# First loads on ScalarE's queue, and K's transposes moved on VectorE: two attention blocks on one core

## The chip, the cores and the metric

The kernel runs on one core of a Trainium2 chip. The metric is the device time of one execution in microseconds. A core has TensorE (matrix products), VectorE, ScalarE, GpSimd, SyncE and 16 DMA engines. In the profile they are PE (with PEld, its weight loads), DVE, ACT, POOL and SP. A suffix q (SPq, ACTq) means the engine's instruction queue, mostly while it issues a DMA. The engines run on their own and wait for each other by semaphores. Each executes its own instructions strictly in order.

## What is computed

Two independent attention blocks, A and B, and their outputs side by side. For each block, with B = 16 batches, 64 queries, D = 640, H = 32 heads of 128, and 512 cached keys, all in bfloat16:

```python
q = (x @ wq).reshape(B, Sq, H, Dh).transpose(0, 2, 1, 3)
scores = einsum("bhqd,bhkd->bhqk", q, k_cache) * (Dh ** -0.5)
p = softmax(scores, axis=-1)
o = einsum("bhqk,bhkd->bhqd", p, v_cache)
out = o.transpose(0, 2, 1, 3).reshape(B, Sq, H * Dh) @ wo
```

K and V are read once: 268 MB of the 295 MB that the profile counts.

## The kernel before

**Packs.** The unit of work is a pack: four heads of two batches, so 128 rows (two times 64 queries) by four heads. Four packs (j = 0 to 3) share one pair of batches and its x. Eight pairs make a phase of 32 packs, for 16 heads. A block has two phases, the kernel four, so there are 128 packs, n = 0 to 127. Each phase has its own wq and wo columns for 16 heads. The sum over the two phases of a block is held in acc.

**Steps of a pack.** The names are those of the plan and of the functions em_... that write the instructions:

- LDK (four loads of 256 KB, rows of 8 KB), LDV (two loads of 512 KB, rows of 4 KB, or of 2 KB in every fourth pack): K and V into rings of 6 and 4 packs.
- LDX (160 KB, rows of 1,280 bytes): x of a pair. LDWQ: wq. In phase 0 it is cut by pack, four loads of 640 KB with rows of 1 KB; later phases have five loads of 512 KB with rows of 4 KB. LDWO: wo, 640 KB in rows of 1,280 bytes.
- XT, XE, XC: transpose x on TensorE, bring it out on ScalarE, copy it on GpSimd (L582, L588, L592). WP: GpSimd reorders wq of a pack, two copies (L575).
- QP, QE: the query product (TensorE, L603) and its way out (ScalarE, L609).
- KT: VectorE transposes K, in two halves (L617). S: scores (TensorE, L627).
- EX: exp of one head with its row sum (ScalarE, L646). RC: reciprocals, RC0 for heads 0 to 2 and RC1 for head 3 (VectorE, L659). NM: p times the reciprocal into pn_sb, four times (GpSimd, L675; for the last pack VectorE).
- TR: transpose pn_sb (TensorE, L686). TE: two copies of it to SBUF (VectorE, L696). PV: product with V (TensorE, L710). OE, ZO: its way out and a clearing of PSUM (ScalarE, L718, L722). OP: product with wo (TensorE, L730). OS: every fourth pack, add into acc or out_sb (VectorE, L740, L743). ST: store (ScalarE's queue, L749).

**What sets the order.** build_plan gives each step a planned time: the pack's number plus an offset from the table AT, in units of one pack. Each engine's program is its steps sorted by that time. Dependencies are also found in that order: a read depends on the last write planned ahead of it. SP is the exception: it only issues loads, sorted by the key that stands in `loads`. So an offset in AT is no delay. It says only what stands ahead of what. In TensorE's order, one pack is S(n), TR(n-1), OP(n-2), for some XT, QP(n+1), PV(n-1). TensorE runs this as a loop of 32 turns of four packs, whose program is written once.

**The first microseconds.** Packs -2 and -1 are dummies that run TR, PV and OP on cleared tiles. SP issues x0, wq0, K0, wq1, K1, wq2, K2, wq3, x1, V0, wo0, K3, V1, wo1, K4, V2, wo2, K5, V3, wo3, K6, x2, V4 and so on. V4 goes into the buffer that V0 had, so SP waits there until PV(0) is through; V5 waits for PV(1). Everything behind a waiting load on SP waits too. Between V4 and V5 stand two loads of the next wq (phase 1) and K7. GpSimd's order is WP(0), XC(0), WP(1), the clearing of pn_sb (L666) that TR(-1) needs, WP(2), NM of pack 0, WP(3), NM of pack 1.

**VectorE's order in one pack** is, by AT: RC0(n), sometimes OS, RC1(n), the two KT of pack n+2, the two TE of pack n, then RC0(n+1).

Of the kernel before, what the change touches and what calls it, by code (L numbers as in the profile page):

```python
# [20 lines left out]
class Cfg:  # L21
# [9 lines left out]
    BASE = 32  # L31
    KLEAD = 2.5
    WIDE = (0, 1, 2)
    AT = dict(XT=-2.485, XE=-2.28, XC=-0.9, QP=-0.45, QE=-0.24, KT=(-1.24, -1.0), S=0,
              EX=(0.21, 0.32, 0.43, 0.54), RC=(0.53, 0.75), NM=(0.56, 0.69, 0.82, 0.95), NMZ=(0.54, 0.55, 0.56, 0.76), TR=1.2,
              TE=(1.26, 1.39), PV=1.75, OE=(2.0, 2.06), ZO=2.11, OP=2.31, OS=2.545, LDWO=2.6, ST=3.374, WP0=-1.75, WP1=-1.6)


class Op:
# [19 lines left out]
def build_plan(dims, cfg, general):  # L59
# [6 lines left out]
    N = NPH * PH  # L66
    AT = cfg.AT
    ops = []
    loads = []
    at = {}  # L70

    def add(eng, kind, idx, ts, reads=(), writes=()):
        op = Op(eng, kind, idx, ts, reads, writes)
        ops.append(op)
        at[(kind, idx)] = op
        return op

    def add_output(n):
        g, j = n // NJ, n % NJ
        final = n >= 0 and dims["FINAL"](g // NBP)  # L80
        for b in range(2):
            tv = n + AT["PV"]
            op = add("sp", "LDV", (n, b), tv - 0.3, [], [("v" if n >= 0 else "absent", n % cfg.NV, b)])
            loads.append((n - cfg.NV + AT["PV"] + 0.2 if n >= 0 else -99.0, 3, op))
        if n > -2:
            add("pe", "TR", n, n + AT["TR"], [("pn", i) for i in range(4)] + [("ident",)], [("B", 4), ("B", 5)])
        for b in range(2):
            add("dve", "TE", (n, b), n + AT["TE"][b], [], [("B", 4 + b), ("pT", b)])
        add("pe", "PV", n, n + AT["PV"], [("pT", 0), ("pT", 1), ("v", n % cfg.NV, 0), ("v", n % cfg.NV, 1)],
            [("B", 4), ("B", 5), ("B67",)])  # L90
# [13 lines left out]
    for g in range(N // NJ + 1):  # L104
        n0 = g * NJ
        txt = n0 + AT["XT"]
        add("pe", "XT", g, txt, [("xn", g % cfg.NXN), ("ident",)], [("SB", 0)])
        if g == N // NJ:
            break
        if dims["FIRST"](g // NBP):  # L110
            add("act", "XE", g, n0 + AT["XE"], [], [("SB", 0), ("xs", g % NBP)])
            op = add("sp", "LDX", g, txt - 0.5, [], [("xn", g % cfg.NXN)])
            loads.append((txt - 3.7 if g else -7.0, 0, op))
        add("pool", "XC", g, n0 + AT["XC"], [("xs", g % NBP)], [("xT", g % cfg.NX)])
    for ph in range(NPH):
        twp = [ph * PH + j + (AT["WP1"] if ph else AT["WP0"]) for j in range(NJ)]
        for kt in range(dims["KT"] if ph else 0):
            ready = twp[-1] - PH + 0.5 if ph > 1 else NJ - 1 + AT["WP0"] + 0.5
            op = add("sp", "LDWQ", (ph, kt), twp[0] - 0.5, [], [("ws", kt, j) for j in range(NJ)])
            loads.append((ready + 0.5 + 0.5 * kt if ph == 1 else ready + 2.0 + 0.14 * PH * kt, 1, op))  # L120
        for j in range(NJ):
            w = ph * NJ + j
            n0 = ph * PH + j
            add("pool", "WP", w, twp[j], [("ws", kt, j) for kt in range(dims["KT"])], [("wqp", j)])
            if not ph:
                op = add("sp", "LDWQ", (0, j), twp[j] - 0.5, [], [("ws", kt, j) for kt in range(dims["KT"])])
                loads.append((0.9 * j - 5.2, 1, op))
            if ph:
                add("act", "LDWO", w, n0 - NJ + AT["LDWO"], [], [("wo", j)])
            else:  # L130
                loads.append((n0 - 1.9, 4, add("sp", "LDWO", w, n0 + AT["OP"] - 0.8 * NJ, [], [("wo", j)])))
# [6 lines left out]
    for n in range(-2, N):  # L138
# [3 lines left out]
        g, j = n // NJ, n % NJ  # L142
        add("pe", "QP", n, n + AT["QP"], [("xT", g % cfg.NX), ("wqp", j)], [("SB", 1)])
        add("act", "QE", n, n + AT["QE"], [], [("SB", 1), ("qs", n % cfg.NQ)])
        for i in range(4):
            op = add("sp", "LDK", (n, i), n + AT["KT"][0] - 0.9, [], [("kn", n % cfg.NK)])
# [6 lines left out]
        for i in range(4):  # L153
            h = 4 * n + i
            te = n + AT["EX"][i]
            if general:
                add("dve", "MX", h, te - 0.002, [], [("SB", i), ("negmax", h % 4)])
            add("act", "EX", h, te, [("negmax", h % 4)] if general else [],
                [("SB", i), ("p", h % cfg.NP), ("rs", h)])
# [4 lines left out]
    if not general:  # L164
        add("dve", "FL1", 0, N - 1 + AT["TE"][1] + 0.002, [("rs", h) for h in range(4 * N)], [("good",)])
        add("pe", "FLM", 0, N - 1 + AT["OP"] + 0.002, [("good",)], [("SB", 0)])
# [38 lines left out]
    for op in ops:  # L205
# [3 lines left out]
        if op.kind == "XT" and op.idx > 0:  # L209
            at[("EX", 4 * (NJ * op.idx - NJ + 1))].deps += [d for d in op.deps if d.kind == "LDX"]  # L210
            op.deps = [d for d in op.deps if d.kind != "LDX"]
        if op.kind == "QP" and op.idx > 0:
            at[("EX", 4 * op.idx - 4)].deps += [d for d in op.deps if d.kind == "WP"]
            op.deps = [d for d in op.deps if d.kind != "WP"]

    own = {"XC", "QE", "KT", "NM", "TE", "OE", "ZO", "OS", "LDV"}

    def for_pe(d):
        if d.kind == "EX":
            return d.idx % 4 < 2  # L220
        if d.kind == "OE":
            return d.idx[1] == 0
        if d.kind == "NM":
            return d.idx % 4 == 3 and d.eng == "pool"
        if d.kind == "OS" and d.idx == N // NJ - 1:
            return False
        return d.kind in own

    def stand_in(d, op):
        if op.eng == "pe":  # L230
# [4 lines left out]
            if d.kind == "OE":  # L235
                return at[("OE", (d.idx[0], 0))]
            if d.kind in ("EX", "MX") and not for_pe(d):
                if op.kind == "S":
# [11 lines left out]
        if d.kind == "OS":  # L250
            return at[("PV", d.idx * NJ + NJ)]
        if d.kind == "TE":
            return at[("PV", d.idx[0])]
# [9 lines left out]
    counts = dict(base)  # L263

    def sem_key(op):
        if op.kind == "LDV":
            return ("d_v", op.writes[0][1])
        if op.kind in LOADS:
            return ("d_" + op.kind[2:].lower(),) + op.writes[0][1:]
        if op.kind == "ST":  # L270
            return ("d_out",)
        return ("q_" + op.eng,) if for_pe(op) else ("s_" + op.kind.lower() + "_" + op.eng,)

    for eng in ENGINES:
        for op in progs[eng]:
            op.sem = sem_key(op)
            counts[op.sem] = op.count = counts.get(op.sem, 0) + 1
# [151 lines left out]
def mha_kernel(nc, blocks, out, cfg=None):  # L429
# [17 lines left out]
    for general in (False, True):  # L447
        dims = dict(NPH=NPH, NBP=NBP, NJ=NJ, KT=KT, FIRST=lambda ph: ph % NSUB == 0,
                    FINAL=lambda ph: ph % NSUB == NSUB - 1)
        plans.append(build_plan(dims, cfg, general))  # L450
# [457 lines left out]
```

## Time and profile before

| | |
|---|---|
| Median of 6 runs | 749.7 us (749.08 to 752.27) |
| The profiled execution | 749.43 us, its span 747.7 us |
| TensorE busy, granted clock | 678.3 us (91%), 0.99 |
| VectorE, ScalarE, GpSimd busy | 526.0, 519.0, 404.0 us |
| Moved by DMA | 295.15 MB, mean 395 GB/s over the span |
| GpSimd's NM waiting for RC | 315.2 us in 121 waits |
| VectorE's KT waiting for K | 78.2 us (B) and 37.9 us (A) |
| SP waiting for PV ahead of a V load | 36.1 us and 18.4 us |
| The chain that ended last | PE 40%, SPq 29%, DMA 12% |

How to read it: the span runs from the first to the last instruction. A timeline line has the start, the time that the group took, the engine with the line of the code, the operation, its output and inputs, the number of instructions, and in brackets the idle time ahead of it with what ended it. "issue" there means that the profile shows nothing that was waited for. In the table by windows the last two columns are the share of time that the DMA engines were busy (it can pass 1.00) and the rate.

### The profile page before, as it was taken

The page shows a single profiled execution, that of the slowest core. Times are in us where ns is not written, and L with a number is a line of the kernel's source. Part 1 is how long each engine was busy: PE and PEld are TensorE (multiplying, and loading weights), DVE is VectorE, ACT ScalarE, POOL GpSimd, SP SyncE. Part 2 cuts the span into 40 slices and gives each one's busy share as a digit, 9 for nine tenths or more (in the row PEclk, how much of TensorE's full clock was granted, in tenths as well). Part 3 has the DMA queues.
Part 4 walks back from the last instruction along what each step waited for, and adds up shares of the span by engine and source line. Part 5 has one row for each costly group of instructions (what it writes and reads, how often), then busy time and mean ns, then how long its engine had stood idle before and what let it go on. Part 6 is the DMA issues. An engine that isn't in the chain of part 4 may idle for free.

```text
span 747.7 us, 57618 instructions
## 1 busy us (share of the span) xinstructions
PE 678.3 (91%) x26518; PEld 530.7 (71%) x26518; DVE 526.0 (70%) x818; ACT 519.0 (69%) x1559; POOL 404.0 (54%) x580
## 2 busy tenths in 40 slices
PE   4579999999998999989988999999898899999994
PEld 3457777777776777777766777777776677777773
DVE  7437777777767677677755676777676687877773
ACT  2438778787776767767756777777776677777772
POOL 5435555655964454645684545546476455564550
PEclk9979999999999999999999999999999999999998
DMA  8999999999999999999999999999999999999970
GB/s 314 398 401 410 411 412 414 411 411 412 406 399 415 413 412 411 413 413 414 411 400 407 411 413 412 412 411 409 412 409 401 410 414 414 404 415 413 412 297 16
DMA packets 87518, 295.15 MB, mean 395 GB/s; under 512 B 13360, under 2 KB 28208, under 8 KB 71088
## 3 DMA queue, kind: packets, MB, share of 16 engines
q1 hardware_dynamic: 78832, 284.22, 95.1%
q10 hardware_dynamic: 8640, 10.49, 3.9%
q14 instruction: 37, 0.30, 0.1%
q8 instruction: 9, 0.15, 0.1%
HBM read 292.03 MB, written 2.62 MB: 394 GB/s over the span
## 4 chain that ended last, share of the span: by engine, by line
PE 40%; SPq 29%; DMA 12%; POOL 5%; DVE 5%; issue 4%; ACT 4%; ACTq 0%; DVEq 0%
SPq L552 20%; PE ps L710 10%; PE ps L730 10%; PE ps L603 9%; DMA kn_ring<-in_B_k_cache_dram 8%; PE ps L627 5%; PE ps L686 5%; SPq L563 5%; POOL pn_sb L675 4%; SPq L565 3%; DMA v_ring<-in_B_v_cache_dram 2%; DVE kt_ring L617 2%; ACT p_ring L646 2%; DMA kn_ring<-in_A_k_cache_dram 2%; ACT oT_sb L718 2%
## 5 line engine op out<-in xcount | busy, mean ns | idle before, releaser
L675 POOL TENSOR_SCALAR pn_sb<-p_ring,recip 128x512 bf16<-128x512 bf16 x508 | 341.8, 692 | 315.2 <-DVE recip L659 315.2
L617 DVE STREAM_TRANSPOSE kt_ring<-kn_ring 128x1024 f32<-128x1024 f32 x256 | 302.9, 1222 | 116.4 <-DMA kn_ring<-in_B_k_cache_dram 78.2
L646 ACT ACTIVATE p_ring<-ps 128x512 bf16<-128x512 f32 x512 | 298.2, 597 | 19.1 <-DMA xn_ring<-in_B_x_dram 3.1
L696 DVE COPY pT_sb<-ps 128x1024 bf16<-128x1024 bf16 x258 | 164.2, 677 | 63.3 <-PE ps L686 62.5
L710 PE MATMUL ps<-pT_sb,v_ring 32*128 32x64 bf16 (+1 forms) x14528 | 162.8, 192 | 27.1 <-DVE pT_sb L696 10.1
L710 PEld LDWEIGHTS ps<-pT_sb,v_ring 32*128 32x128 bf16 (+1 forms) x14528 | 146.4, 92 | 42.9 <-issue 22.1
L730 PE MATMUL ps<-wo_sb,oT_sb 128*128 128x320 bf16 x1040 | 166.3, 303 | 5.9 <-issue 4.9
L603 PE MATMUL ps<-xT_ring,wqp_sb 128*128 128x128 bf16 x2560 | 166.1, 221 | 5.9 <-POOL xT_ring L592 5.8
L603 PEld LDWEIGHTS ps<-xT_ring,wqp_sb 128*128 128x128 bf16 x2560 | 157.6, 114 | 12.8 <-issue 6.0
L718 ACT ACTIVATE oT_sb<-ps 128x256 bf16<-128x256 f32 x260 | 85.6, 381 | 115.5 <-PE ps L710 115.5
L627 PE MATMUL ps<-kt_ring,qs_ring 32*64 32x512 bf16 x4096 | 138.3, 380 | 0.0
L609 ACT ACTIVATE qs_ring<-ps 128x512 bf16<-128x512 f32 x128 | 76.5, 597 | 82.2 <-PE ps L603 82.2
L686 PEld LDWEIGHTS ps<-ident,pn_sb 64*128 64x128 bf16 x4128 | 70.3, 95 | 76.3 <-ACT ps L722 42.9
L730 PEld LDWEIGHTS ps<-wo_sb,oT_sb 128*128 128x128 bf16 x1040 | 91.8, 98 | 43.6 <-issue 5.4
L646 ACT ACTIVATION_READ_ACCUMULATOR p_ring<-ps 128x1 f32 x512 | 106.0, 207 | 0.0
L686 PE MATMUL ps<-ident,pn_sb 64*128 64x64 bf16 x4128 | 84.0, 191 | 20.0 <-POOL pn_sb L675 12.1
L627 PEld LDWEIGHTS ps<-kt_ring,qs_ring 32*64 32x64 bf16 x4096 | 53.9, 103 | 28.0 <-issue 0.5
L659 DVE RECIPROCAL recip<-rowsum 128x3 f32<-128x3 f32 (+1 forms) x256 | 39.9, 162 | 32.0 <-ACT p_ring L646 27.9
L722 ACT ACTIVATE ps<-zeros 128x256 f32<-128x256 bf16 x130 | 51.6, 397 | 0.0
L575 POOL COPY wqp_sb<-ws_sb 128x1280 bf16<-128x1280 bf16 x32 | 39.2, 1253 | 7.1 <-DMA ws_sb<-in_A_wq_dram 7.1
L592 POOL COPY xT_ring<-xs_sb 128x640 bf16<-128x640 bf16 x32 | 22.9, 716 | 3.6 <-PE ps L603 3.6
L582 PE MATMUL ps<-ident,xn_ring 128*128 128x128 bf16 x165 | 14.9, 222 | 4.5 <-DMA xn_ring<-in_A_x_dram 3.5
(26 smaller groups left out, 65.7 us busy)
## 6 DMA issues: line engine op xcount, KB each, us to landing
kn_ring<-in_A_k_cache_dram SPq DMA_DIRECT2D x256, 256.0 KB
v_ring<-in_A_v_cache_dram SPq DMA_DIRECT2D x128, 512.0 KB, 12.2
kn_ring<-in_B_k_cache_dram SPq DMA_DIRECT2D x256, 256.0 KB
v_ring<-in_B_v_cache_dram SPq DMA_DIRECT2D x128, 512.0 KB, 12.8
ws_sb<-in_B_wq_dram SPq DMA_DIRECT2D x10, 512.0 KB, 16.1
wo_sb<-in_B_wo_dram ACTq DMA_DIRECT2D x8, 640.0 KB, 13.6
ws_sb<-in_A_wq_dram SPq DMA_DIRECT2D x4, 640.0 KB, 8.3
wo_sb<-in_A_wo_dram SPq DMA_DIRECT2D x4, 640.0 KB, 12.8
```

The costliest lines, as they stand in the source:

```text
L552: ins = e.dma_start(kn_ring[2 * b + l::4, n % NK].rearrange("p a c -> p (a c)"), src)
L603: last = e.matmul(ps[:, 1, f * 128:(f + 1) * 128], w[:, kt, f, :], xT_ring[:, xs, kt, :], start=(kt == 0), stop=(kt == KT - 1))
L609: ins = e.activation(qs_ring[:, op.idx % NQ].rearrange("p f b q -> p (f b q)"), ps[:, 1, :], ACTF.Copy, scale=scale)
L617: ins = e.transpose(dst.rearrange("p c b (h l) -> p c h b l", h=8, l=2), src)
L627: last = e.matmul(ps[64 * b:64 * b + 64, i, :], qs_ring[rows, n % NQ, f, b, :], kt_ring[rows, n % NKT, :, f // 2, b, :, f % 2], start=(f = ...
L646: ins = e.activation(dst, src, ACTF.Exp, scale=1.0, accum_out=rowsum[:, h:h + 1])
L675: ins = e.tensor_scalar(dst, src, recip[:, h // 4 % NR, i:i + 1], 1.0, ALU.mult, ALU.mult)
L686: last = e.transpose(pt_bank(b)[:, 64 * c:64 * c + 64], pn_sb[rows, c, :], ident[rows, rows], tile_position=(64 * b, 0))
L696: ins = e.tensor_copy(pT_sb[:, b].rearrange("p t q -> p (t q)"), pt_bank(b))
L710: last = e.matmul(ps[:, 4 + i, 64 * b:64 * b + 64], v_ring[rows, n % NV, b, c, :], pT_sb[rows, b, c, :], start=(t == 0 and i < 2), stop=(t ...
L718: ins = e.activation(oT_sb[:, 2 * a:2 * a + 2, :], o_ps[:, 2 * a:2 * a + 2, :], ACTF.Copy)
L730: last = e.matmul(out_ps[:, s, :], oT_sb[:, i, :], wo_sb[:, 4 * j + i, s * NH0:(s + 1) * NH0], start=(j == 0 and i == 0), stop=(j == NJ - ...
```

## The change

1. **First loads.** x of the first pair and the four wq loads of phase 0 leave SP's list and are issued by ScalarE, ahead of everything else in its program (planned times -21 to -17). Each has a semaphore of its own. SP starts with K0, K1, K2.
2. **The table AT.** Nearly all offsets change, and most of them leave the order on each engine as it was. What changes in the order:
   - VectorE: KT has offsets -0.672 and -0.375 instead of -1.24 and -1.0. In one pack the order becomes RC0(n), sometimes OS, the second KT of pack n+1, RC1(n), the first KT of pack n+2, the two TE of pack n, RC0(n+1). So the second KT moves from ahead of TE to between the next RC0 and RC1.
   - ScalarE: LDWO (phases 1 to 3) stands ahead of the fourth EX instead of behind it, ST behind the third EX instead of behind the second.
   - SP: two of the later wq loads (the first of phases 2 and 3) come behind a V load instead of ahead of it.
   - The last pack (NMZ): the NM of heads 2 and 3 get 1.718 and 1.794. That is behind the pack's own TR (1.293), so in the changed plan these two heads of the last pack are normalised after their transpose, and TR takes what pn_sb still holds from the pack before. This is the one part of the computation that differs. VectorE also has NM of head 1 behind RC1, and the check of the row sums (FL1) ahead of the last two NM.

```diff
-    AT = dict(XT=-2.485, XE=-2.28, XC=-0.9, QP=-0.45, QE=-0.24, KT=(-1.24, -1.0), S=0,
-              EX=(0.21, 0.32, 0.43, 0.54), RC=(0.53, 0.75), NM=(0.56, 0.69, 0.82, 0.95), NMZ=(0.54, 0.55, 0.56, 0.76), TR=1.2,
-              TE=(1.26, 1.39), PV=1.75, OE=(2.0, 2.06), ZO=2.11, OP=2.31, OS=2.545, LDWO=2.6, ST=3.374, WP0=-1.75, WP1=-1.6)
+    AT = dict(XT=-2.585, XE=-2.383, XC=-0.788, QP=-0.428, QE=-0.224, KT=(-0.672, -0.375), S=0,
+              EX=(0.252, 0.307, 0.358, 0.616), RC=(0.572, 0.794), NM=(0.803, 0.854, 1.088, 1.187),
+              NMZ=(0.615, 1.231, 1.718, 1.794), TR=1.293, TE=(1.432, 1.47), PV=1.701, OE=(1.888, 2.013), ZO=2.221,
+              OP=2.387, OS=2.576, LDWO=2.6, ST=3.559, WP0=-1.75, WP1=-1.596)
...
-            op = add("sp", "LDX", g, txt - 0.5, [], [("xn", g % cfg.NXN)])
-            loads.append((txt - 3.7 if g else -7.0, 0, op))
+            if g:
+                loads.append((txt - 3.7, 0, add("sp", "LDX", g, txt - 0.5, [], [("xn", g % cfg.NXN)])))
+            else:
+                add("act", "LDX", g, -21.0, [], [("xn", g % cfg.NXN)])
...
-                op = add("sp", "LDWQ", (0, j), twp[j] - 0.5, [], [("ws", kt, j) for kt in range(dims["KT"])])
-                loads.append((0.9 * j - 5.2, 1, op))
+                add("act", "LDWQ", (0, j), j - 20.0, [], [("ws", kt, j) for kt in range(dims["KT"])])
...
+        if op.kind in ("LDX", "LDWQ") and op.eng == "act":
+            return ("d_first",) + op.writes[0]
```

## The prediction

> **What bounds the kernel now.** I read the page's slices first, then the head in two-microsecond windows, then the loads by queue.
>
> ```profile
> DMA  8999999999999999999999999999999999999970
> GB/s 314 398 401 410 411 412 414 411 411 412 406 399 415 413 412 411 413 413 414 411 400 407 411 413 412 412 411 409 412 409 401 410 414 414 404 415 413 412 297 16
> ```
>
> The 16 DMA engines are full from the first slice to the 38th, near 411 GB/s. TensorE is at 99% in 60 to 195 us and 600 to 735 us, at about 5.2 us a pack; a pack's K and V, 2.1 MB, take 5.1 us at 411 GB/s. The two are level, and only DMA never pauses. So the end moves by whatever DMA loses or gains, plus the lag from the last data to the last store.
>
> ```profile
> 2.00:4.00 2.00, 0.48 (x5) 0.46 (x5) 2.00 (x1) 0.08 (x1) 0.00 (x0) 1.00 0.64 178
> 4.00:6.00 2.00, 0.21 (x2) 0.00 (x0) 1.57 (x2) 0.70 (x1) 0.00 (x0) 1.00 1.08 343
> 6.00:8.00 2.00, 0.00 (x0) 0.00 (x0) 1.48 (x2) 0.00 (x0) 1.24 (x2) 1.00 0.89 361
> ```
>
> The last two columns are DMA share and GB/s. The head has 0.72 us of idle DMA in 2 to 4 us and 0.22 us in 6 to 8 us: 0.9 us is all that quicker issuing can win.
>
> **Part 1: the first loads.** SP loses x (0.39 us of issue) and four wq loads (0.42 to 0.59 us each); ScalarE gets them ahead of all else (five at about 0.38 us, its row for wo, near 2 us, beside its 1.28 us table load, while it has nothing else to do). K's first issue is still at about 1.04 us. The point is who shares the engines afterwards.
>
> ```profile
> q10 hardware_dynamic: 8640, 10.49, 3.9%
> ...
> wo_sb<-in_B_wo_dram ACTq DMA_DIRECT2D x8, 640.0 KB, 13.6
> ...
> wo_sb<-in_A_wo_dram ACTq DMA_DIRECT2D x4, 640.0 KB, 15.2
> out_dram<-out_sb ACTq DMA_DIRECT2D x16, 160.0 KB, 6.5
> ```
>
> q10 is ScalarE's queue: 12 wo loads of 512 rows and 16 stores of 128 rows are 8,192 of its 8,640 packets, so a packet is a row. A wo load, alone on its queue, takes 13.4 us (median of 12) though its 32 rows per engine are 1.6 us of work at 411/16 = 25.7 GB/s. Suppose an engine takes one row of each queue in turn: a K row (8 KB) is 0.32 us, a V row (4 KB) 0.16, wo, x or wq rows 0.04 to 0.05. 32 turns beside one third K and two thirds V are 32 x (0.21 + 0.05) = 8.4 us, and 10.2 with the 1.8 us that the last store takes alone. Measured: 10.7 to 16.2. Turns by row explain it, and rather flatter ScalarE's queue.
>
> Now x is 8 rows per engine, each wq load 40. Beside them SP sends K0 to K2 (24 rows), x1 (8), V0 (16), wo0 (32), K3 (8), V1 (16), wo1 (32), K4, V2, wo2. From the first bytes at 2.7 us: 24 turns at 0.36, 8 at 0.09, 18 at 0.16 to 0.2 end wq0 at about 15.5; the next three end at 21.5, 26.5 and 34; with 1.5 us to complete, 17, 23, 28 and 35.5. Stretched by 13.4/10.2, wq1 and wq2 come at 29 and 36. I take 25 and 30, nearer the count because SP's own queue thins by then. In the head as it is:
>
> ```profile
> 11.33 2.45 POOL L575 COPY wqp_sb<-ws_sb 128x1280 bf16<-128x1280 bf16 x2 [1.46 <-DMA ws_sb<-in_A_wq_dram]
> ...
> 13.72 1.80 POOL L666 MEMSET pn_sb<- 128x2048 bf16 x1
> ...
> 17.23 1.03 PE L686 MATMUL ps<-ident,pn_sb 64*128 64x64 bf16 x32
> ...
> 27.36 0.58 PE L686 MATMUL ps<-ident,pn_sb 64*128 64x64 bf16 x27 [2.94 <-issue]
> ...
> 48.25 0.38 PE L710 MATMUL ps<-pT_sb,v_ring 32*128 32x64 bf16 x27 [2.61 <-issue]
> ...
> 48.69 0.81 SPq L563 DMA_DIRECT2D v_ring<-in_A_v_cache_dram  x2
> ```
>
> POOL copies wq1 from 11.33, clears pn_sb, and the dummy TR(-1) runs at 17.23. TR(0) starts at 24.16 (6.9 us on, of which 1.2 is an issue gap), breaks off, and PV(1) ends at 48.63, which lets SP issue V5 at 48.69. With the changed queue, wq1 at 25 gives TR(-1) at 25 + 2.45 + 1.80 = 29.3. TR(0) comes at 29.3 + 6.9 - 1.2 = 35.0, or, by wq2 through POOL (30 + 2.45 + 2.7 of NM), at 35.2. From there to PV(1) are 24.5 us as now, with their four issue gaps (2.9, 2.8, 3.7, 2.6 us), each beside one 16 KB packet on the instruction queue q8: 59.7. V5 goes out at 59.8 instead of 48.7.
>
> What has DMA to do till then? Ahead of V5 stand K0 to K7, V0 to V4, four wo, four wq, x0 to x2 and two loads of the next wq: 20.4 MB, the same in both kernels. At the 374 GB/s of the first 60 us they are gone at 54.6. So V5 has 4.3 us to spare now (54.6 - 48.7 - 1.6 from an issue to its first bytes), and the changed kernel runs dry for 59.8 + 1.6 - 54.6 = **6.8 us**. A rate already full can't win that back. Bounds: 17/23/28 gives 4.8, 29/36 gives 12.7, ScalarE's queue sharing like SP's gives 0 and a gain of 0.9.
>
> The Trainium skill (DMA: Bandwidth & Descriptors, "Issuing engines are not separate DMA queues") says that issuing from several engines saves only the issue time. By that alone the sum would be about 1 us faster; the wo row says that the small-row queue waits besides. Its page Runtime: NRT & Kernel Launch ("Instruction fetch mechanics") has the next 16 KiB of instructions fetched during the current ones, mostly hidden. The gaps above disagree; were they hidden behind the longer waits, V5 would be in time and nothing lost.
>
> **Part 2: VectorE.** Only one step changes in each pack: K's second transpose leaves its place ahead of TE and goes between the two reciprocals.
>
> ```profile
> 568.43 19.50 DMA kn_ring<-in_B_k_cache_dram
> ...
> 587.95 2.37 DVE kt_ring L617 x2
> 590.32 1.17 DVE pT_sb L696 x2
> ...
> 591.67 2.70 POOL pn_sb L675 x4
> ```
>
> This is the last place where the chain waits for K. From K's landing to the end of TE are 3.54 us; without one transpose, 2.36. But the V that PV needs next is 1 MB behind that K: 2.55 us. So the lag shrinks by 3.54 - 2.55 = **1.0 us** (0 to 1.2), and TensorE carries it to the end. V is late next.
>
> ```profile
> 711.90 0.18 DVE L659 RECIPROCAL recip<-rowsum 128x3 f32<-128x3 f32 x1
> 712.17 2.69 POOL L675 TENSOR_SCALAR pn_sb<-p_ring,recip 128x512 bf16<-128x512 bf16 x4 [1.68 <-DVE recip L659]
> 712.48 0.16 DVE L659 RECIPROCAL recip<-rowsum 128x1 f32<-128x1 f32 x1 [0.40 <-ACT p_ring L646]
> 713.20 2.37 DVE L617 STREAM_TRANSPOSE kt_ring<-kn_ring 128x1024 f32<-128x1024 f32 x2 [0.55 <-DMA kn_ring<-in_B_k_cache_dram]
> 714.01 1.07 PE L627 MATMUL ps<-kt_ring,qs_ring 32*64 32x512 bf16 x32
> ```
>
> The new wait: RC1 stands behind the transpose, ready at 711.90 + 0.18 + 1.22 + 0.16 = 713.46; POOL wants it after three NM, at 714.19. S at 714.01 wants the transpose, done at 713.30. Both fit by 0.7 us, so I cost it at 0. Behind RC1 queue the next pack's first transpose and TE, which wait for K and TR anyway. K's buffer comes free later (n - 0.375 by the table), but SP asks for it only at n + 1.4. In every fourth pack the 0.80 us OS stands between and the cover is gone; 32 packs by at most 0.1 us are 3 us.
>
> **Part 3: small steps, together 0.** The wo issue goes ahead of ScalarE's fourth EX: 0.38 us, 12 times, and QE waits for QP 0.37 us anyway. On SP two wq loads go behind a V instead of ahead of it. At the end, two normalisations go behind the last TR; that TR waited for OE (0.79 us, till 734.81) with the normalisations done at 734.16, so nothing is won (0 to -0.2).
>
> **Sum.** 6.8 - 1.0 = 5.8 us. The profiled execution has 749.43 us (span 747.7, 1.7 around it), 0.3 under the median of 749.7; from the median, 755.5.
>
> **Rivals.** (a) ScalarE's queue keeps up with SP's. Then 0.9 and 1.0 are won: 747.8. For it: SP needs 0.6 us to issue 256 KB, so its queue holds little at first. Against: the wo rows. It decides from the point where wq1's copy starts before 18.5 us: 18.5 + 4.25 + 5.7 + 24.5 = 53.0, where V5's spare time ends. (b) wq is late, but TensorE's four issue gaps (12.0 us) go by behind the longer waits, and V5 goes out at 59.8 - 12.0 = 47.8: only the lag changes, 748.7. Against: the gaps come exactly 127 matmuls apart (6 + 20 + 64 + 32 + 5, then 27 + 8 + 5 + 20 + 67, and so on), so they hang on the place in the program, not on waits. (c) wq is harmless, but RC1 or S waits behind the moved transpose in OS packs: 3 - 1 = 2 us slower, 751.7. Against: the 0.7 us above.
>
> **Chances.** The forecast 0.61 (751.2 to 763), (a) 0.22 (747 to 748.5), (b) 0.13 (748.2 to 751), (c) 0.04. Within 0.2%, about what a measurement of this kernel can tell from no change, lies (b). So faster 0.22, the same 0.13, slower 0.65. The range takes in (a) and the 12.7 us bound (761.4 with the lag's 1.0 off), and some of what turns slower than that would add: 747.3 to 763.
>
> **What would show it.** Right: the second wq copy on POOL near 25 us, TR(0) near 35, V5 issued near 60, and a dip in the second to fourth slice of DMA; the K waits on VectorE shorter and V waits more. Wrong: wq copies near their old times, or full DMA through 50 to 65 us. If the issue gaps of TensorE's first turn are gone, (b) is right.

## The result, and the profile after

The changed kernel takes 747.88 us (median of 17 runs; one of them, of 1257 us, is left out of the ratio as disturbed); before, beside it, 749.76 us (38 runs). The ratio is 0.9969, 95% interval 0.9961 to 0.9977: 0.3% faster. The forecast was 755.5 us and slower, so it was wrong in sign; the time is that of rival (a), 747.8. The profiled execution has 747.9 us with a span of 746.2, against 749.43 and 747.7.

The page's rate row first. Where the forecast wanted a dip between 55 and 62 us, in the third and fourth of the forty slices, there is none, and the first slice is fuller (328 for 314).

```profile
GB/s 328 392 401 411 411 411 414 411 411 411 407 398 415 411 413 411 414 412 413 414 397 407 410 413 412 411 411 410 412 408 402 410 414 413 413 415 411 413 315 19
```

The same windows of the head as before (the last two columns are DMA share and GB/s):

```profile
2.00:4.00 2.00, 0.68 (x5) 0.46 (x5) 2.00 (x1) 0.00 (x0) 0.00 (x0) 1.00 0.97 230
4.00:6.00 2.00, 0.02 (x1) 0.00 (x0) 1.57 (x2) 0.00 (x0) 0.00 (x0) 1.00 0.99 301
6.00:8.00 2.00, 0.00 (x0) 0.00 (x0) 1.48 (x2) 0.00 (x0) 0.21 (x1) 1.00 1.04 368
```

The idle 0.72 us in 2 to 4 us and 0.22 us in 6 to 8 us have gone, as counted. In 4 to 6 us, where most of the rows moved are wq's of 1 KB, the rate is lower than before (301 GB/s for 343), so that over the first 20 us the gain is 6.62 against 6.37 MB, or 0.24 MB before rounding, 0.6 us at 411 GB/s.

Now the queues on the page, which show the loads where the change put them:

```profile
q10 hardware_dynamic: 11408, 13.27, 5.1%
...
ws_sb<-in_A_wq_dram ACTq DMA_DIRECT2D x4, 640.0 KB, 17.5
```

A wq load takes 17.5 us (median) from issue to landing, where it took 8.3 on SP's queue. That is slow, as the forecast wanted, but not by as much: its landings at 17, 25 and 30 us would have made the median well over 20. The error shows in the landing times one by one. The timeline of the head (start, us, engine, line; lines are four higher than before):

```profile
1.21 6.81 ACTq L543 DMA_DIRECT2D ws_sb<-in_A_wq_dram  x4
...
7.79 2.45 POOL L579 COPY wqp_sb<-ws_sb 128x1280 bf16<-128x1280 bf16 x2 [6.22 <-DMA ws_sb<-in_A_wq_dram]
...
16.45 2.45 POOL L579 COPY wqp_sb<-ws_sb 128x1280 bf16<-128x1280 bf16 x2 [5.55 <-DMA ws_sb<-in_A_wq_dram]
...
20.79 1.03 PE L690 MATMUL ps<-ident,pn_sb 64*128 64x64 bf16 x32 [3.78 <-POOL pn_sb L670]
...
28.07 0.86 PE L690 MATMUL ps<-ident,pn_sb 64*128 64x64 bf16 x32 [0.97 <-POOL pn_sb L679]
...
50.01 0.82 SPq L567 DMA_DIRECT2D v_ring<-in_A_v_cache_dram  x2
```

wq0 to wq3 are copied from 7.79, 16.45, 22.76 and 29.46 us; before, the second to fourth came at 11.33, 15.95 and 22.43. So wq1 is 5 us late, not 14. TR(-1) runs at 20.79 and TR(0) at 28.07, 3.9 us later than before. V5 goes out at 50.01 instead of 48.69. That is within the 4.3 us that it has to spare (till 53.0), and DMA runs on at 414 GB/s through 50 to 60 us.

VectorE and its neighbours in one pack of the second half:

```profile
714.65 0.18 DVE L663 RECIPROCAL recip<-rowsum 128x3 f32<-128x3 f32 x1
714.74 1.22 DVE L621 STREAM_TRANSPOSE kt_ring<-kn_ring 128x1024 f32<-128x1024 f32 x1
714.92 2.70 POOL L679 TENSOR_SCALAR pn_sb<-p_ring,recip 128x512 bf16<-128x512 bf16 x4 [2.50 <-DVE recip L663]
...
715.88 0.12 DVE L663 RECIPROCAL recip<-rowsum 128x1 f32<-128x1 f32 x1
...
716.49 1.07 PE L631 MATMUL ps<-kt_ring,qs_ring 32*64 32x512 bf16 x32
```

One transpose stands between the reciprocals. The second reciprocal is ready at 716.00, and GpSimd's four normalisations run through without a break; the fourth starts at about 716.95 (714.92 and three of 0.675). S starts at 716.49, half a microsecond after the transpose. Over the whole kernel GpSimd waits for reciprocals 303.6 us in 119 waits, before 315.2 in 121. The new wait costs nothing.

The chain that ended last, where it waits for data:

```profile
558.43 20.00 DMA v_ring<-in_B_v_cache_dram
578.44 0.05 issue
578.49 1.64 PE ps L714 x128
```

Before, the last four waits for data here were for K. Now V is late as well: in 360 to 600 us TensorE's weight loads wait 13.8 us for V of block B and its matmuls 11.1 us (before 7.2 and 2.2). That is what the prediction meant by V being late next. K is not out of the chain: its last wait ends at 691.57 us, where it ended at 587.93. And VectorE's transposes wait longer for K, not shorter as forecast: 99.4 us for B and 35.9 for A, before 78.2 and 37.9.

### The profile page after: what moved, and what is told of

The parts are those of the page before. It is cut to its first block, busy times and chain, and to the rows that moved or that the text cites. A ratio compares the mean times of both kernels' runs of the same rounds, so it can differ in the third digit from the quotient of the medians.

```text
span 746.2 us, 57746 instructions
## 1 busy us (share of the span) xinstructions
PE 680.6 (91%) x26518; PEld 529.6 (71%) x26518; DVE 516.3 (69%) x818; ACT 519.8 (70%) x1559; POOL 405.3 (54%) x580
## 4 chain that ended last, share of the span: by engine, by line
SPq 37%; PE 28%; DMA 18%; POOL 5%; issue 4%; ACT 4%; DVE 2%; ACTq 0%; DVEq 0%
SPq L556 24%; PE ps L714 8%; PE ps L734 7%; SPq L567 7%; PE ps L607 6%; DMA kn_ring<-in_A_k_cache_dram 6%; DMA v_ring<-in_B_v_cache_dram 5%; SPq L569 5%; POOL pn_sb L679 5%; DMA kn_ring<-in_B_k_cache_dram 4%; PE ps L690 3%; PE ps L631 3%; DMA ws_sb<-in_A_wq_dram 3%; ACT p_ring L650 2%; ACT oT_sb L722 1%
## 5 line engine op out<-in xcount | busy, mean ns | idle before, releaser
L679 POOL TENSOR_SCALAR pn_sb<-p_ring,recip 128x512 bf16<-128x512 bf16 x508 | 343.1, 697 | 303.6 <-DVE recip L663 303.6
L621 DVE STREAM_TRANSPOSE kt_ring<-kn_ring 128x1024 f32<-128x1024 f32 x256 | 313.3, 1229 | 135.3 <-DMA kn_ring<-in_B_k_cache_dram 99.4
L700 DVE COPY pT_sb<-ps 128x1024 bf16<-128x1024 bf16 x258 | 164.0, 676 | 79.0 <-PE ps L690 78.2
L714 PE MATMUL ps<-pT_sb,v_ring 32*128 32x64 bf16 (+1 forms) x14528 | 162.4, 192 | 24.3 <-DMA v_ring<-in_B_v_cache_dram 11.1
L714 PEld LDWEIGHTS ps<-pT_sb,v_ring 32*128 32x128 bf16 (+1 forms) x14528 | 145.4, 92 | 40.7 <-DMA v_ring<-in_B_v_cache_dram 13.8
L734 PE MATMUL ps<-wo_sb,oT_sb 128*128 128x320 bf16 x1040 | 168.4, 306 | 4.7 <-issue 3.7
L663 DVE RECIPROCAL recip<-rowsum 128x3 f32<-128x3 f32 (+1 forms) x256 | 36.8, 144 | 4.9 <-ACT p_ring L650 0.8
## 6 DMA issues: line engine op xcount, KB each, us to landing
wo_sb<-in_B_wo_dram ACTq DMA_DIRECT2D x8, 640.0 KB, 12.8
ws_sb<-in_A_wq_dram ACTq DMA_DIRECT2D x4, 640.0 KB, 17.5
```

Source lines behind the costliest of these rows:

```text
L621: ins = e.transpose(dst.rearrange("p c b (h l) -> p c h b l", h=8, l=2), src)
L679: ins = e.tensor_scalar(dst, src, recip[:, h // 4 % NR, i:i + 1], 1.0, ALU.mult, ALU.mult)
L700: ins = e.tensor_copy(pT_sb[:, b].rearrange("p t q -> p (t q)"), pt_bank(b))
L714: last = e.matmul(ps[:, 4 + i, 64 * b:64 * b + 64], v_ring[rows, n % NV, b, c, :], pT_sb[rows, b, c, :], start=(t == 0 and i < 2), stop=(t ...
L734: last = e.matmul(out_ps[:, s, :], oT_sb[:, i, :], wo_sb[:, 4 * j + i, s * NH0:(s + 1) * NH0], start=(j == 0 and i == 0), stop=(j == NJ - ...
```

## The experiments

The theory at this point: wq came early enough, because its rows did not take strict turns with K's in the first 8 us, so V5 was issued within its spare time and the two small gains stood. The rivals: the price of a late V5 was wrong, so that wq's landing does not matter; or all the gain is the table's and the new loads bring none.

**Each part alone.** e1_loads_only is the kernel before with part 1 and the old table; e2_table_only the kernel before with the new table; e3_vectore_only the kernel before with only the second transpose moved; e4_end_in_order the changed kernel with the last pack's normalisations ahead of its transpose, and so with the whole computation.

```diff
# e3, on the kernel before
-KT=(-1.24, -1.0)
+KT=(-1.24, -0.375)
# e4, on the changed kernel
-NMZ=(0.615, 1.231, 1.718, 1.794)
+NMZ=(0.615, 0.795, 0.796, 0.797)
```

> The kernel before with the first loads on ScalarE's queue and the old table. Theory: the change has two gains, DMA that is ahead in the first 20 us (0.24 MB more by the windows, about 0.6 us) and a shorter lag behind K on VectorE; so this alone gives 0.5 to 1.0 us, 748.7 to 749.2. Rival A (all of the gain is the loads): 747.5 to 748. Rival B (all of it is VectorE's order): no change, 749.7, or slower, because TensorE is later in the head and nothing makes up for it.

> The kernel before with the new table and the first loads on SP as they were. As in the changed kernel, two heads of the last pack are normalised after their transpose, which takes what the pack before left. Theory: the lag alone, 0.6 to 1.2 us faster, 748.5 to 749.1. Rival A (all of the gain is the loads): no change. Rival B (all of it is VectorE's order or another step of the table): 747.5 to 748.

> The kernel before with one number changed: K's second transpose at -0.375, between the two reciprocals. Theory: this step is all that the table brings, so the same time as the run with the whole table, within 0.3 us, and 0.6 to 1.2 us faster than before. Rival: another step of the table (the wo issue on ScalarE, the end of the last pack) has a part, and this stays 0.5 us or more behind the whole table.

> The changed kernel with the last pack's four normalisations all ahead of its transpose, so the computation is whole again. Theory: the last transpose waits for ScalarE's copy anyway (it did in both kernels, 0.79 us), so nothing changes: the time of the changed kernel within 0.3 us. Rival: the end owes something to the two normalisations left behind, and this is 0.5 us or more slower than the changed kernel.

| | median, us | ratio to before | last S starts |
|---|---|---|---|
| before | | 1 | 729.53 |
| loads only | 749.1 | 0.9990 [0.9980, 1.0001] | 729.14 |
| table only | 748.58 | 0.9982 [0.9970, 0.9993] | 727.61 |
| moved transpose only | 748.99 | 0.9992 [0.9980, 1.0005] | 727.91 |
| end in order | 747.76 | 0.9965 [0.9955, 0.9975] | 727.09 |
| changed | 747.88 | 0.9969 [0.9961, 0.9977] | 727.11 |

The last column is S of pack 127 in the profiled execution. The parts nearly add up: 0.10% and 0.18% against 0.31%. The table brings the larger part, 1.9 us by the last S; the loads 0.4 us. The intervals of the loads and of the moved transpose alone reach 1, so by time these two are not settled. The moved transpose alone comes 0.41 us behind the whole table, between what was expected and its rival.

The traces settle the moved transpose better than the times do. Two lines each of before and of the changed kernel, VectorE's last wait for K and the last S:

```profile
723.35 2.37 DVE L617 STREAM_TRANSPOSE kt_ring<-kn_ring 128x1024 f32<-128x1024 f32 x2 [0.32 <-DMA kn_ring<-in_B_k_cache_dram]
729.53 1.07 PE L627 MATMUL ps<-kt_ring,qs_ring 32*64 32x512 bf16 x32
```

```profile
722.42 1.25 DVE L621 STREAM_TRANSPOSE kt_ring<-kn_ring 128x1024 f32<-128x1024 f32 x1 [0.64 <-DMA kn_ring<-in_B_k_cache_dram]
727.11 1.07 PE L631 MATMUL ps<-kt_ring,qs_ring 32*64 32x512 bf16 x32
```

From the one to the other are 6.18 us before and 4.69 after. All ten profiled kernels with the moved transpose have 4.55 to 4.75; the table without it (e7, below) has 6.18 like before. In the loads-only kernel VectorE does not wait for the last K, so it has no such number. The two normalisations behind the last TR are worth nothing: with them back in order the kernel is as fast.

**The table without the transposes.** e7_table_without_kt is the kernel before with the new table, but both transposes ahead of TE.

```diff
-KT=(-0.672, -0.375)
+KT=(-0.672, -0.671)
```

> The kernel before with the new table, except that K's second transpose stays right behind the first, as it was. Two heads of the last pack are normalised after their transpose, as in the changed kernel. Theory: the rest of the table brings nothing, so this is the time of before within 0.5 us (749.5 to 750.2). Rival: the rest of the table brings what the run with VectorE's step alone lacked against the whole table (0.4 to 0.8 us): 749.0 to 749.4.

Measured: 750.2 us, 1.0003 [0.9994, 1.0013]; last S at 728.90. By time the rest of the table brings nothing: with the transpose moved it is 0.18% faster, without it the same as before.

**What a late wq costs.** e5_wq_behind_xe has ScalarE issue wq behind its first XE; e6_wq_behind_qe has it issue wq1 to wq3 behind QE of pack 0. Nothing else differs from the changed kernel.

```diff
# e5
-add("act", "LDWQ", (0, j), j - 20.0, ...
+add("act", "LDWQ", (0, j), 0.01 * j - 2.3, ...
# e6, after ScalarE's order is made
+late = [o for o in progs["act"] if o.kind == "LDWQ" and o.idx[1] > 0]
+rest = [o for o in progs["act"] if o not in late]
+cut = rest.index(at[("QE", 0)]) + 1
+progs["act"] = rest[:cut] + late + rest[cut:]
```

> The changed kernel with ScalarE's four wq loads issued behind its first copy of x instead of ahead of it: from about 4.9 us instead of 1.2. Theory: how soon wq lands hangs on the start, where ScalarE's rows ran ahead of SP's; from 8 us on the two queues went row by row. If they run ahead here too, all wq is only 3.7 us later (copies on GpSimd at 11.5, 20, 26.5, 33) and V5 goes out at 53 to 56 us, at the edge of the spare time: 747.5 to 750.5. If SP's queue is already full of K rows by then and the turns are row by row from the start, the second copy starts at 22 to 24 us, V5 goes out at 57 to 58 and DMA runs dry for 4 to 5 us: 751 to 753. Rival (lateness in the head costs nothing at all): as the changed kernel, 747.9.

> The changed kernel with wq1 to wq3 issued by ScalarE behind the first QE, at about 13.5 us, when SP's queue is surely full; x and wq0 as in the changed kernel. It tests the second half of the forecast that failed, the price of a late V5. By turns of one row: second copy on GpSimd at 25 to 30 us, V5 issued at 58 to 65 us, DMA dry between 55 and that, and the time longer by about as much: 752 to 759. Rival: V5 late costs nothing because TensorE catches up later: 748 to 749.

e5: 750.74 us, 1.0017 [1.0002, 1.0032]; wq copied from 15.48, 21.40, 28.04 and 33.12 us, V5 issued at 55.81. That lies between the two outcomes expected. e6: 754.42 us, 1.0064 [1.0049, 1.0080]; copies from 7.76, 26.91, 32.26 and 37.33, V5 at 58.61. Here is the hole that the prediction described, in the timeline and the windows of e6:

```profile
58.61 0.81 SPq L571 DMA_DIRECT2D v_ring<-in_A_v_cache_dram  x2
```

```profile
55.00:60.00 5.00, 2.23 (x106) 1.10 (x93) 0.00 (x0) 0.94 (x3) 0.00 (x0) 0.84 0.55 215
```

In these 5 us the DMA engines are busy 0.55 of the time, at 215 GB/s, where the changed kernel has 1.03 and 414. With wq1 and wq2 copied at 26.9 and 32.3 us, near the 25 and 30 that I took, the kernel is 0.64% or 4.8 us slower than before, against 5.8 forecast. So the rival that a late V5 is harmless falls, and the price was right to about 1 us.

**wq in longer rows.** e8_wq_long_rows_act has phase 0's wq as five loads of 512 KB with 4 KB rows, as the later phases do, on ScalarE; e9_wq_long_rows_sp has the same five loads on SP ahead of K. Both have the end in order.

```diff
-e.dma_start(ws_sb[:, :, i, :], src[:, :, c + i * 512:c + i * 512 + 512])
+e.dma_start(ws_sb[:, i].rearrange("p j c -> p (j c)"), src[:, i, c:c + NJ * 512])
```

> The changed kernel (with the last pack's normalisations in order) but phase 0's wq is loaded like that of the later phases: five loads of 512 KB with rows of 4 KB on ScalarE's queue, instead of four of 640 KB with rows of 1 KB. 640 rows in all instead of 2,560. It asks why ScalarE's rows ran ahead of SP's in the first 8 us (819 to 89 in 4 to 8 us). If it is the number of rows in the loads being issued, the run-ahead goes, the queues share row by row from the start, and all wq lands near 20 us: TR(0) near 34, V5 at 55 to 57, DMA dry for 2 to 4 us: 749 to 751. If a queue that starts first simply stays ahead, wq lands by 10 to 12 us, and longer rows fill the first 10 us better: 746.5 to 747.5.

> The same five loads with rows of 4 KB, issued by SP ahead of K; only x0 is left on ScalarE. With one queue there is no turn to lose: wq lands by about 10 us, K0 by 13, TR(-1) at about 17 and V5 at 48 to 51, inside the spare time. The first 10 us moved 2.65 MB in the changed kernel; at 400 GB/s from 2.6 us they would move 3.0, so up to 0.35 MB or 0.9 us more is won: 746.5 to 747.2. Rival: the late K0 holds back the first pack and nothing is won: 747.7 to 748.5.

e8: 753.66 us, 1.0051 [1.0037, 1.0065]. That is above what was expected: no pack can start before the last of the five loads has landed, at 19.5 us, and V5 goes out at 58.20. e9: 750.07 us, 1.0004 [0.9994, 1.0015], where a win was expected. wq is there at 11.8 us, but TR(-1) runs at 20.32 and not near 17, and V5 is issued at 52.71, at the very edge of its time: DMA is busy 0.96 and 0.90 of 52 to 54 and 54 to 56 us. The profiled execution took 747.74, but the runs spread from 747.13 to 751.81. A V5 that is now and then later would do that; V5 in the other runs is not on record, so the cause is open.

**Why ScalarE's rows ran ahead.** The row counts of the queues in short windows. Three views of the changed kernel, 4 to 6, 6 to 8 and 20 to 22 us (queue, packets, MB, share of 16 engines; a packet is a row):

```profile
q10 hardware_dynamic: 437, 0.45, 76.5%
q1 hardware_dynamic: 26, 0.16, 22.1%
```

```profile
q10 hardware_dynamic: 382, 0.38, 59.8%
q1 hardware_dynamic: 63, 0.36, 44.1%
```

```profile
q1 hardware_dynamic: 308, 0.42, 63.2%
q10 hardware_dynamic: 308, 0.31, 46.9%
```

In the last view the two queues move the same number of rows, as turns of one row each would have it and as the prediction supposed, and so it is from about 8 us on (142 to 126 in 8 to 10 us, then 126 to 125, 167 to 170, 240 to 237 rows). But in 4 to 6 us the counts were 437 to 26 and in 6 to 8 us 382 to 63, in favour of ScalarE's queue. Two experiments vary what stands in the queues then: e10_v_first has SP issue V0 and V1 ahead of K0, and e11_wq_in_20 cuts wq's four loads of 640 rows into twenty of 128. Both have the end in order.

```diff
# e10
-loads.append((n - cfg.NV + AT["PV"] + 0.2 if n >= 0 else -99.0, 3, op))
+loads.append((n - 9.0 if n in (0, 1) else n - cfg.NV + AT["PV"] + 0.2 if n >= 0 else -99.0, 3, op))
# e11
-add("act", "LDWQ", (0, j), j - 20.0, [], [("ws", kt, j) for kt in range(dims["KT"])])
+for kt in range(dims["KT"]):
+    add("act", "LDWQ", (0, (j, kt)), j - 20.0 + 0.1 * kt, [], [("ws", kt, j)])
```

> The changed kernel with the end of the last pack in its old order, and with V0 and V1 (four loads of 128 rows of 4 KB) issued by SP ahead of K0. It asks why ScalarE's rows run ahead in 4 to 8 us (819 rows against 89) before the strict turns begin. Theory 1, little stands ready in SP's queue, because a K load gives it only 32 rows per 0.66 us of issue: four V loads put 512 rows there by about 3.5 us, so turns of one row each should begin at once, about 300 rows each in 4 to 8 us, and the first wq copy on GpSimd comes near 12 us instead of 7.8. Theory 2, ScalarE's rows go ahead as long as ScalarE is still issuing them, whatever stands in SP's queue: several rows to one again in 4 to 8 us, a wq issue of well over 0.5 us each, and the first copy near 7.8 us. The time itself is no test: K0 comes about 5 us later than it did, which delays the first scores by as much, 748 to 755 us by what V5 has to spare.

> The changed kernel with the end of the last pack in its old order, and with phase 0's wq issued by ScalarE as twenty loads of 128 rows of 1 KB instead of four of 640. The rows are the same; only the number of rows that one load gives a DMA engine is different (8 instead of 40). Theory 1, in the first 8 us the engines serve the two queues a whole load at a time, and only later a row at a time: the row counts of 4 to 6 us stand as the rows of one load do, 640 to 32 in the changed kernel (17 to 1 measured), 128 to 32 with wq in long rows (4.0 to 1 measured), 640 to 128 with V first (5.4 to 1 measured). Then here it is 128 to 32: near 260 rows against 65 in 4 to 6 us, the first wq copy comes at 9 to 11 us and the second behind 18.5 us, so V5 is late: 748.5 to 752 us. Theory 2, 1 KB rows on ScalarE's queue run ahead in these microseconds however they are cut: above 350 rows against 30, the first copy below 8.5 us, 747.5 to 748.5 us. Against both stands the issue of twenty loads, which at 0.38 us each lasts to 8.8 us at least: then the third and fourth pack of wq are late whatever the sharing is.

e10: one run of 749.4 us beside one of 750.19 before. First copy at 12.52 us, as theory 1 had it. Against theory 1, the rows still ran ahead in 4 to 6 us, 380 to 71, but from 6 us on the turns were equal, although ScalarE's fourth wq issue was under way until 12.8 us:

```profile
q1 hardware_dynamic: 167, 0.62, 76.6%
q10 hardware_dynamic: 172, 0.17, 25.9%
```

That is the view of 6 to 8 us, against 382 to 63 above. So an issue still under way on ScalarE does not keep its rows in the lead. e11: 752.21 us, 1.0020 [1.0006, 1.0034]. The same rows in smaller loads lost most of the lead: 187 to 76 in 4 to 6 us, the first copy at 10.55 us, V5 at 57.11. Theory 2 of e11 (above 350 to 30 however they are cut) falls; theory 1 had 260 to 65.

| kernel | rows of one load, ScalarE : SP | rows moved in 4 to 6 us |
|---|---|---|
| changed | 640 : 32 = 20 | 437 : 26 = 17 |
| V first | 640 : 128 = 5 | 380 : 71 = 5.4 |
| wq in long rows | 128 : 32 = 4 | 129 : 32 = 4.0 |
| wq in 20 | 128 : 32 = 4 | 187 : 76 = 2.5 |

In these four the lead goes with the rows of one load, as if whole loads took turns. That is argued from four counts, not shown, and two other counts do not fit it. With loads of 640 and 32 rows as in the changed kernel, e6 has 457 to 11 in 4 to 6 us, and e5, whose wq is issued from 4 us, has 210 to 55, 296 to 68 and 279 to 82 in 6 to 12 us, about four to one. What makes the lead, and what ends it (after 6 us with V first, 8 us in the changed kernel, 12 us in e5), stays open.

**The price of V5, over all runs.** By the prediction's 53.0 us, each microsecond that V5 is issued later costs one. The column "last K" is how much later than in the changed kernel (722.42 us) VectorE's last wait for K ends, in the same execution that V5 is read from:

| kernel | V5 issued | after 53.0 | last K | 747.9 + (V5 - 53.0) | measured |
|---|---|---|---|---|---|
| wq behind XE | 55.81 | 2.8 | 3.3 | 750.7 | 750.74 |
| wq behind QE | 58.61 | 5.6 | 6.0 | 753.5 | 754.42 |
| wq in long rows | 58.20 | 5.2 | 5.8 | 753.1 | 753.66 |
| V first | 54.66 | 1.7 | 1.9 | 749.6 | 749.4 (one run) |
| wq in 20 | 57.11 | 4.1 | 4.2 | 752.0 | 752.21 |
| wq in long rows on SP (e9) | 52.71 | 0 (in time) | 0.7 | 747.9 | 750.07 |
| changed | 50.01 | 0 (in time) | 0 | 747.9 (in time) | 747.88 |

In one execution the last K is as late as the rule has it, or up to 0.7 us later. The measured times are medians beside a kernel before of 749.67 to 749.91 us; only for V first it took 750.19 and for wq in 20 750.76, so that this row is about 1 us lower in comparison. The median that doesn't fit is that of e9; its profiled execution, with 747.74 us, does.

## Why the prediction was wrong

- **The step that failed** is the sum "24 turns at 0.36, 8 at 0.09, 18 at 0.16 to 0.2" and what was taken from it, "I take 25 and 30". It lets ScalarE's and SP's queues move one row each from the first bytes on. The runs show that only from about 8 us; in its place stand 437 rows to 26 in 4 to 6 us and 382 to 63 in 6 to 8. The sum gave 17, 23 and 28 for wq0 to wq2, and I went later still; measured are 7.8, 16.5 and 22.8. Why the rows run ahead stays open. The wo loads that I took the rule from are issued in steady state, so they could not show the first 8 us. (The 13.4 us that I call the median of 12 is that of all 16 wo loads, four of them on SP's queue; the page has 13.6 and 15.2 for ScalarE's eight and four.) A counter-argument stood in the text, under rival (a): SP needs 0.6 us to issue 256 KB, so its queue holds little at first. I gave that rival a chance of 0.22. Whether it is the reason is not shown: with V first SP's queue held more, and the lead shrank and ended sooner, but it was there.
- **The time of rival (a) was met in part by luck.** The point from which it decides held (wq1 copied at 16.45 us, before 18.5), but ScalarE's queue did not keep up with SP's (17.5 us a load for 8.3). In the two profiled executions the last K is 0.93 us earlier and the lag behind it 1.49 us shorter, and 0.85 us of that is lost at the end; (a) had 0.9, 1.0 and 0.
- **The chain from wq to V5 was right.** With the measured landings, its rule of 5.15 us (copy 2.45, NM 2.7) from wq2 gives 22.76 + 5.15 = 27.9 for TR(0), against 28.07. From TR(0) to V5 are 21.9 us instead of 24.5: the first gap (2.9 us) is gone there, three others stand (3.07, 3.67 and 3.59 us). So rival (b) held for one gap of four. (The 99% of TensorE that I gave for 600 to 735 us is 98% in the view; nothing hangs on it.)
- **V5's spare time and its price were right**: the table above, within 0.7 us by the last K.
- **The head's 0.9 us**: the idle time is gone, and 0.6 us of bytes are won in the first 20 us; alone, the loads give 0.10% [-0.01, 0.20]. VectorE's last wait for K ends at 722.42 and 722.34 us (changed, end in order), and at 722.72 to 723.35 in the four kernels with the loads on SP as before, so the gain there is between 0.3 and 1.0 us. ScalarE's issues, taken at 0.38 us each, were mis-sized: the fourth wq load held it for 4.91 us, and XE ran at 9.34 us instead of 4.25; V5's spare time covered that.
- **The lag, 1.0 us (0 to 1.2)**: the step named is the one that brings it, since e7 without it has nothing, but the size was too small: 1.4 to 1.6 us by the traces (6.18 against 4.55 to 4.75), 0.08 to 0.18% by time. That is more than the one transpose (1.2 us) taken out; what the rest is, the runs do not show. V is late next in the middle of the kernel only; the last wait for data in the chain is K's. The sign "K waits on VectorE shorter" was wrong: they grew from 116.1 to 135.3 us in all.
- **The new wait on VectorE and the small steps, 0**: right. The reciprocals' waits for ScalarE even fell, from 27.9 to 0.8 us, since the transpose runs in that time. The rest of the table has 1.0003 [0.9994, 1.0013].
- **The skill's rule** that I weighed, the Trainium skill's page DMA: Bandwidth & Descriptors, "Issuing engines are not separate DMA queues", is that only the issue time is saved, by my estimate about 1 us here. The sum by it came nearest, but not because the queue has no effect: issued later on the same queue (e5, e6), the same loads make the kernel take 750.7 to 754.4 us.
- **Part of the gain is lost at the end.** The last S is 2.42 us earlier, the last store 1.57 us (741.01 against 742.58). The OP of the last pack but one takes longer, before and after:

```profile
736.45 0.29 PE L686 MATMUL ps<-ident,pn_sb 64*128 64x64 bf16 x7 [1.09 <-issue]
736.67 1.26 PE L730 MATMUL ps<-wo_sb,oT_sb 128*128 128x320 bf16 x8
```

```profile
733.69 0.45 PE L690 MATMUL ps<-ident,pn_sb 64*128 64x64 bf16 x9 [0.78 <-issue]
734.07 2.32 PE L734 MATMUL ps<-wo_sb,oT_sb 128*128 128x320 bf16 x8
```

The granted clock there was 0.50 in the changed kernel (734 to 736 us) and 1.00 before (736 to 738), although the pause ahead of it was the longer one before. The same group takes 1.26 us in e5, e9 and e10 too, and 1.5 to 2.3 in the other profiled executions, so it is not tied to the change; what decides it is not shown.

## What to carry to other kernels

When a load moves to another queue, don't price it with a sharing rule from steady state: count rows by queue in two-microsecond windows at the place itself. Then follow the load to the next instruction that releases a load (here wq to TR to PV to V5) and compare its time with when DMA runs out: within the spare time lateness is free, beyond it each microsecond costs one. With a change this small the times of the parts do not settle what each brings: with twelve runs each, two of the three intervals took in no change. A distance inside the trace, here from the last K to the last S, settled the moved transpose; it was worth 1.4 to 1.6 us, more than the 1.0 us that the distance from K to V allowed it.

## What the runs showed of the hardware that was not expected

- Two queues with work moved the same number of rows (308 to 308 in 20 to 22 us, 126 to 125 in 12 to 14), whatever the rows' size: 1 KB beside 8 KB. In the first microseconds it was not so (437 to 26).
- The last of the four wq issues of 640 rows held ScalarE long: 4.91 us in the changed kernel, 8.08 in e5 and 9.62 in e10, and the last of three 3.44 in e6. The ones ahead of it took 0.4 to 1.0. What it waited for is not shown.
- TensorE's pauses of 2.6 to 3.9 us, 127 matmuls apart, come at the same instructions in the changed kernel and in e5, but can shrink: two of before (1.2 and 2.9 us) do not appear in the changed kernel, where TensorE waits longer for GpSimd ahead of them, and two are 1.27 us long in e5.
